# Second matmul of the expert network follows the first by three half steps instead of four and five, with its passes dealt out anew

## The chip, the cores and the metric

The kernel runs on one core of a Trainium2 chip. The core has five engines with instruction queues of their own, each worked off in order: TensorE (PE, matmuls into PSUM), ScalarE (ACT), VectorE (DVE), GpSimd (POOL) and SyncE (SP, which here issues the DMAs). Engines wait for each other by semaphores. The metric is the device time of one execution in microseconds: the median of three executions before the change is 485.01 us (484.96 to 485.11).

## The reference

Two blocks follow each other. A linear attention with a polynomial sketch gives x of 4352 tokens by 128; a mixture of four experts then works on all tokens:

```python
def phi(x):
    a = np.einsum('rd,bhsd->bhsr', S1, x)
    b = np.einsum('rd,bhsd->bhsr', S2, x)
    return np.einsum('bhsi,bhsj->bhsij', a, b).reshape(*x.shape[:-1], r * r)
q_p, k_p = (phi(q), phi(k))
kv = np.einsum('bhsf,bhsd->bhfd', k_p, v)
z = np.sum(k_p, axis=2)
attn = np.einsum('bhsf,bhfd->bhsd', q_p, kv) / (np.einsum('bhsf,bhf->bhs', q_p, z)[..., None] + 1e-06)
# (B,H,S,D) -> x: (B*S, H*D) = (4352, 128)
p = domain_probs / (domain_probs.sum(-1, keepdims=True) + 1e-09)
for e in range(4):
    h = np.maximum(x @ w1[e], 0.0)          # (4352, 1024)
    out += p[:, e:e + 1] * (h @ w2[e])      # (4352, 128)
```

B, H, S, D are 4, 4, 1088, 32, r is 8; all data are fp32.

## The kernel before

The tokens are columns. They are cut into eleven chunks (`CHUNKS`, L71): chunk 0 has 128 columns, chunk 1 has 448, chunks 2 to 7 have 512 each, then 320, 256 and 128. Each chunk passes all four experts, and of each expert the 1024 hidden rows in eight blocks of 128. Two blocks make a **step**, so an expert has four steps (`NP`) and a chunk sixteen (`NQ`); the loop at L1084 runs over all steps, numbered through: step 32 is the first of chunk 2. In a step, `f` (0 to 3) is the place in its expert and `j` (0 or 1) the block.

One step issues the first product of its own two blocks, x @ w1, in `first` (L861), and the second product, h @ w2, of an earlier step, in `second` (L945). `LA` = 2: before the change, step i carries the second product of step i - 2. Between the two blocks of `first` a callback `between` is called, so a step has a **middle** (after block 0) and an **end** (after block 1). The middle takes block 0 of step i - 2, the end block 1. If step i - 2 is its expert's last, step i is a **closing step**: the middle takes both blocks, `close` (L1077) gathers the result, and the loop goes on at once with `continue`, with nothing at its end.

Chunks 0 and 10 (`plain`) and chunk 1 (`whole`) work in fp32. In chunks 2 to 9 the fp32 products are put together from single-pass fp32r matmuls on operands that are split into parts. For the first product (any block): L911 (wa, xa) and L912 (wb, xb) into a PSUM bank, then ACT scales the bank in place (L913), and a block later `third` (L926) adds L931 (wd, xd). Then comes the relu. For even blocks (`in_three`) it makes three parts: ha by ACT (L935), hb by DVE (L936), hc by DVE (L937, listed as `hd` in the profile). For odd blocks ACT makes one fp32 tile `hid` (L943). The second product of an even block is L994 (va, ha) and L995 (vb, hb) into a first output bank o0, and one pass (vd, hc) into a second bank o1 by L1001; that of an odd block is an fp32 matmul, issued as two instructions, into o1, by L1001 too. Passes into o1 wait in a list `o1_next` until block 1 of a step when k is 0, otherwise they are issued at once.

`gather` (L1022) closes an expert: ACT copies o0, scaled, to the tile `ev` (L1030), DVE adds o1 (L1031), POOL multiplies by the gate and adds to `total` (L1035, L1037, L1038). It is a generator that is drawn on by `next(ending)` at the end of steps that aren't closing: first it loads the gates of the next chunk (L340), and for the last expert, two draws later, `turn_back` (L1006) has DVE turn the total into the tile `ob` (L1010) and SP store it by four DMAs (L1013).

The tiles `ev` and `ob` have one buffer each. `scaled` (L702) uses the same two, under the tags "ev" and "ob", for casts by ACT (L706) that POOL reads (L710). That is how the split weights are made: `weight_parts` and `second_weight_parts` are spread by `to_part` over steps 16 to 39, after `first` and ahead of what comes at the step's end. The last two casts of this kind stand in step 36. Four steps ahead of a chunk's end `token_parts` (L753) splits the next chunk's x in the same manner.

The attention (`front`, `keys`, `queries`, `attend`) is cut into pieces, which `work()` deals out after each block of `first`, at a rate worked out from what later chunks need. They put matmuls on PE (L226, L410, L666) and products, shuffles and transposes on DVE (L425, L535, L669 to L679), and DMAs on SP (x goes out to DRAM at L643 and back into a ring at L652). All order is the order of the program: the schedule is manual, and each engine takes its instructions as they are written.

Of the kernel before, what the change touches and what calls it, by code (L numbers as in the profile page):

```python
# [8 lines left out]
F32 = mybir.dt.float32  # L9
# [4 lines left out]
ACTF = mybir.ActivationFunctionType  # L14
# [10 lines left out]
def kernel(  # L25
# [24 lines left out]
    nc = tc.nc  # L50

    P = 128
    HP = 64
    B, H, S, D = q.shape
    E, DM, F = w1.shape
# [5 lines left out]
    FB = F // P  # L61
    NQ = E * FB // 2
    QW = 512
    CW = 512
    GE = 160
    LA = 2
    SK, KS = 2, 1
# [11 lines left out]
    mpool = ctx.enter_context(tc.tile_pool(name="moe", bufs=2))  # L79
# [66 lines left out]
    def second_weight(e, b):  # L146

        at = split_at(b)
        return w2_of[e, 0 if in_three(b) else 1][:, DM * at : DM * (at + 1)]

    def in_three(b):
        return b % SK < KS

    def split_at(b):
        return (b % SK - (0 if in_three(b) else KS)) * NK + b // SK
# [540 lines left out]
    R12 = 2.0 ** -12  # L696
# [28 lines left out]
    w2_parts = {}  # L725
# [111 lines left out]
    steps = [(m, kq) for m in range(NC) for kq in range(NQ)]  # L837
    hid, acc, total = {}, {}, {}
    NP = FB // 2

    def plain(m):
        return m in (0, NC - 1)
# [102 lines left out]
    def second(i, j=None):  # L945

        m, kq = steps[i]
        n, (e, f) = CHUNKS[m], divmod(kq, NP)
        hd = hid[i] if j == 0 else hid.pop(i)
        if plain(m):  # L950
# [3 lines left out]
            for j in range(2):  # L954
                for _ in range(2):
# [4 lines left out]
                        start=(f == j == 0),  # L960
                        stop=(f == NP - 1 and j == 1),
# [16 lines left out]
        if whole(m):  # L978
            if f == 0 and j == 0:
                acc[m, e] = None, psum(ps_o, f"o{e % 2}")  # L980
            for j in range(2) if j is None else (j,):
                k = 2 * f + j
                o1 = acc[m, e][1][:, 0:n]
                nc.tensor.matmul(o1, second_weight(e, k), hd[j], start=(k == 0), stop=(k == FB - 1))  # L984
            return
        if f == 0 and j in (0, None):
            acc[m, e] = psum(ps_o, "o0"), psum(ps_o, "o1")
        o0, o1 = (o[:, 0:n] for o in acc[m, e])
        for j in range(2) if j is None else (j,):
            k = 2 * f + j  # L990
            if in_three(k):
                w = slice(DM * split_at(k), DM * (split_at(k) + 1))
                (va, vb, vd), (ha, hb, hc) = w2_parts[e], hd[j]
                nc.tensor.matmul(o0, va[:, w], ha, start=(k == 0), stop=False)  # L994
                nc.tensor.matmul(o0, vb[:, w], hb, start=False, stop=(k == FB - SK + KS - 1))  # L995
                o1_next.append((vd[:, w], hc))
            else:
                o1_next.append((second_weight(e, k), hd[j]))
            if k:
                for x, (w, h) in enumerate(o1_next):  # L1000
                    nc.tensor.matmul(o1, w, h, start=(k == 1 and x == 0), stop=(k == FB - 1 and x == len(o1_next) - 1))  # L1001
                o1_next.clear()

    o1_next = []

    def turn_back(m, src):  # L1006

# [14 lines left out]
    def gather(m, e):  # L1022

        n = CHUNKS[m]
        ev = mpool.tile([P, CW], F32, tag="ev", bufs=1, name="ev")
        o0, o1 = acc.pop((m, e))
        if o0 is None:
            nc.scalar.copy(ev[:, 0:n], o1[:, 0:n])
        else:
            nc.scalar.activation(ev[:, 0:n], o0[:, 0:n], ACTF.Copy, scale=1.0 + R12)  # L1030
            nc.vector.tensor_tensor(out=ev[:, 0:n], in0=ev[:, 0:n], in1=o1[:, 0:n], op=ALU.add)  # L1031
        g = gate.pop((m, e))[:, 0:n]
        if e == 0:
            total[m] = mpool.tile([P, CW], F32, tag="total", bufs=1, name="total")
            nc.gpsimd.tensor_tensor(out=total[m][:, 0:n], in0=ev[:, 0:n], in1=g, op=ALU.mult)  # L1035
        else:
            nc.gpsimd.tensor_tensor(out=ev[:, 0:n], in0=ev[:, 0:n], in1=g, op=ALU.mult)  # L1037
            nc.gpsimd.tensor_tensor(out=total[m][:, 0:n], in0=total[m][:, 0:n], in1=ev[:, 0:n], op=ALU.add)  # L1038
        yield
        if not plain(m + 1):  # L1040
            load_gates(m + 1, [e])
        if e == E - 1:
            yield
            yield

            for _ in range(0 if m + 2 < NC else 4):
                yield
            turn_back(m, total.pop(m)[:, 0:n])
# [28 lines left out]
    def close(i):  # L1077

        nonlocal ending
        ended = gather(steps[i][0], steps[i][1] // NP)  # L1080
        next(ended)
        ending = chain(ending, ended)

    for i in range(len(steps) + LA):  # L1084
        if i < len(steps):
# [15 lines left out]
                    credit[0] -= 1  # L1101
                    piece()

            parted = i >= LA and not plain(steps[i - LA][0]) and not plain(m)
            closing = parted and steps[i - LA][1] % NP == NP - 1

            def between(j):

                if closing:
                    second(i - LA)  # L1110
                    close(i - LA)
                else:
                    second(i - LA, j)

            first(i, work, between if parted else None)
            for parts_of in to_part.get(i, ()):
                next(parts_of, None)
            if kq == NQ - 4 and 0 < m < NC - 2:
# [13 lines left out]
        if i == LA:  # L1132

            made_hp[3] = psum(ps_h, "h")
            for c in (0, HP):
                half_columns(3, made_hp[3], c)
        if i >= LA:
            parted = i < len(steps) and parted
            mm, kk = steps[i - LA]
            if parted and closing:  # L1140
                continue
            second(i - LA, 1 if parted else None)
            if kk % NP == NP - 1 and not plain(mm):
                close(i - LA)
            else:
                next(ending, None)

# [1 line left out]
_INS = ["q", "k", "v", "S1", "S2", "moe_domain_probs", "moe_w1", "moe_w2"]  # L1149
# [26 lines left out]
```

## Time and profile before

| what | value |
|---|---|
| median of three executions | 485.01 us |
| profiled execution | 485.2 us |
| its span, first to last instruction | 483.4 us |
| PE busy | 471.4 us (98%) |
| ACT busy | 331.2 us (69%) |
| DVE busy | 327.2 us (68%) |
| POOL busy | 141.9 us (29%) |
| granted TensorE clock | 1.00 |

In a timeline a row has start and duration in us, engine, line, operation, output and inputs, the shape, and in square brackets the idle time before it and what ended it. A matmul's duration overlaps the next one's start, so distances between starts tell what PE takes. A row of the waits says who waited for whom, then the sum in us, how often, and the longest. In the rows by stretch, busy time and number of instructions of PE, weight loads, DVE, ACT and POOL are followed by the granted clock, the mean busy share of the DMA engines, and GB/s. Chunk 2 begins at 81.0 us, chunk 3 at 138.5, chunk 4 at 193.7, chunk 5 at 247.8, chunk 6 at 301.6, chunk 7 at 353.8, chunk 8 (320 columns) at 404.6 and chunk 9 (256) at 437.2, by their first L911.

### The profile page before, as it was taken

To read this page: it belongs to the slowest core of one execution; us is meant where nothing else is said; L and a number is where in the kernel's file an instruction comes from. 1 tells how busy PE (TensorE), PEld (TensorE's weight loads), DVE (VectorE), ACT (ScalarE), POOL (GpSimd) and SP (SyncE) were. 2 spreads that over 40 slices of the span, in tenths; PEclk is the share of its full clock that TensorE was granted. 3 is DMA by queue.
4 is the path that set the end of the run, shared out by engine and by line. 5 is a ranking of instruction groups with operands and counts; after the bars stand their busy time and mean duration, and the time that the engine had idled before them with its cause. 6 is when DMAs were issued, how large, how long until landed. Compare 5 with 4: busy or idle time off the path is not lost.

```text
span 483.4 us, 8071 instructions
## 1 busy us (share of the span) xinstructions
PE 471.4 (98%) x2845; PEld 330.8 (68%) x2845; DVE 327.2 (68%) x615; ACT 331.2 (69%) x696; POOL 141.9 (29%) x149
## 2 busy tenths in 40 slices
PE   8999999989999999999999999999999999999997
PEld 5965555656666676666666676667666666888987
DVE  6833250696877769687887669597877686765652
ACT  4366676876857777676857777676877686888841
POOL 5134478432222124211322124212331032232120
PEclk9999999999999999999999999999999999999999
DMA  7827204411101212411103210013102100120710
GB/s 225 273 69 159 66 22 87 97 42 23 44 23 49 45 44 65 118 24 41 41 23 65 45 33 24 22 17 45 38 24 58 29 14 15 34 57 22 244 34 18
DMA packets 45472, 29.19 MB, mean 60 GB/s; under 512 B 26264, under 2 KB 40952, under 8 KB 45432
## 3 DMA queue, kind: packets, MB, share of 16 engines
q1 hardware_dynamic: 45416, 28.68, 23.6%
q8 instruction: 22, 0.36, 0.3%
q14 instruction: 18, 0.15, 0.1%
q10 hardware_dynamic: 16, 0.00, 0.0%
HBM read 24.42 MB, written 4.24 MB: 59 GB/s over the span
## 4 chain that ended last, share of the span: by engine, by line
PE 66%; DVE 6%; ACT 5%; issue 2%; ACTq 0%; DVEq 0%
PE o L1001 23%; PE h L931 10%; PE h L912 8%; PE h L911 8%; PE o L994 5%; PE o L995 5%; ACT h L913 3%; PE n L226 2%; PE h L226 2%; PE o L226 1%; DVE qp L535 1%; DVE hd L937 1%; DVE kp L425 1%; PE f L666 1%; DVE hb L936 1%
## 5 line engine op out<-in xcount | busy, mean ns | idle before, releaser
L913 ACT ACTIVATE h<-h 128x512 f32<-128x512 f32 (+2 forms) x256 | 138.0, 539 | 100.6 <-PE h L912 91.6
L936 DVE SCALAR_TENSOR_TENSOR hb<-h,ha 128x512 fp32r<-128x512 f32 (+2 forms) x128 | 80.8, 631 | 92.3 <-ACT ha L935 91.8
L911 PE MATMUL h<-xa,wa 128*128 128x512 f32 (+2 forms) x256 | 140.5, 549 | 0.0
L1001 PE MATMUL o<-hid,w_sb 128*128 128x512 f32 (+2 forms) x256 | 119.2, 547 | 0.0
L937 DVE SCALAR_TENSOR_TENSOR hd<-ha,hb 128x512 fp32r<-128x512 f32 (+2 forms) x128 | 98.8, 772 | 8.4
L931 PE MATMUL h<-xd,wd 128*128 128x512 f32 (+2 forms) x256 | 98.3, 384 | 3.2 <-ACT h L913 1.5
L912 PE MATMUL h<-xb,wb 128*128 128x512 f32 (+2 forms) x256 | 94.2, 368 | 0.0
L1037 POOL TENSOR_TENSOR ev<-ev,gate 128x512 f32<-128x512 f32 (+3 forms) x27 | 31.3, 1159 | 153.8 <-DVE ev L1031 153.1
L943 ACT ACTIVATE hid<-h 128x512 f32<-128x512 f32 (+2 forms) x128 | 70.2, 548 | 0.2 <-PE h L931 0.2
L935 ACT ACTIVATE ha<-h 128x512 fp32r<-128x512 f32 (+2 forms) x128 | 69.9, 546 | 0.0
L911 PEld LDWEIGHTS h<-xa,wa 128*128 128x128 f32 x256 | 48.2, 188 | 30.1 <-issue 18.6
L912 PEld LDWEIGHTS h<-xb,wb 128*128 128x128 f32 x256 | 48.3, 189 | 29.3 <-issue 23.6
L931 PEld LDWEIGHTS h<-xd,wd 128*128 128x128 f32 x256 | 48.0, 188 | 23.7 <-ACT h L913 16.0
L1001 PEld LDWEIGHTS o<-hid,w_sb 128*128 128x128 f32 x256 | 45.9, 188 | 8.1
L1001 PE MATMUL o<-hd,vd 128*128 128x512 f32 (+2 forms) x128 | 48.3, 378 | 2.7 <-DVE ev L1031 2.7
L994 PE MATMUL o<-ha,vab 128*128 128x512 f32 (+2 forms) x128 | 50.6, 395 | 0.0
L995 PE MATMUL o<-hb,vab 128*128 128x512 f32 (+2 forms) x128 | 47.4, 370 | 0.0
L1038 POOL TENSOR_TENSOR total<-total,ev 128x512 f32<-128x512 f32 (+3 forms) x27 | 35.4, 1313 | 2.1
L535 DVE TENSOR_TENSOR qp<-qa,qb 64x512 f32<-64x512 f32 (+5 forms) x44 | 33.1, 753 | 1.0
L1035 POOL TENSOR_TENSOR total<-ev,gate 128x512 f32<-128x512 f32 (+3 forms) x9 | 10.5, 1163 | 70.3 <-issue 34.0
L1001 PEld LDWEIGHTS o<-hd,vd 128*128 128x128 f32 x128 | 24.0, 187 | 9.3 <-DVE ev L1031 4.5
L984 PE MATMUL o<-hid,w_sb 128*128 128x448 f32 x64 | 28.9, 544 | 0.0
(150 smaller groups left out, 545.4 us busy)
## 6 DMA issues: line engine op xcount, KB each, us to landing
gate<-gates SPq DMA_DIRECT2D x16, 256.0 KB
kn<-in_k_dram SPq DMA_DIRECT2D x4, 544.0 KB
vn<-in_v_dram SPq DMA_DIRECT2D x16, 128.0 KB
w_sb<-in_moe_w_dram SPq DMA_DIRECT2D x4, 512.0 KB
w_sb<-in_moe_w_dram SPq DMA_DIRECT2D x8, 256.0 KB
w_last<-in_moe_w_dram SPq DMA_DIRECT2D x4, 512.0 KB
gate<-gates SPq DMA_DIRECT2D x8, 224.0 KB
qn<-in_q_dram SPq DMA_DIRECT2D x2, 544.0 KB
```

The source lines that it names most:

```text
L535: nc.vector.tensor_tensor(out=qp[p][64 * x : 64 * x + 64, 0:n], in0=qa[64 * p : 64 * p + 64, 0:n], in1=qb[64 * p : 64 * p + 64, 0:n], op=A ...
L911: nc.tensor.matmul(g, wa[:, e, w], xa, start=True, stop=False)
L912: nc.tensor.matmul(g, wb[:, e, w], xb, start=False, stop=True)
L913: nc.scalar.activation(g, g, ACTF.Copy, scale=1.0 + R12)
L931: nc.tensor.matmul(g, w, x, start=False, stop=True, skip_group_check=True)
L935: nc.scalar.activation(ha, g, ACTF.Relu, scale=NEAR)
L936: nc.vector.scalar_tensor_tensor(out=hb, in0=g, scalar=0.0, in1=high, op0=ALU.max, op1=ALU.subtract)
L937: nc.vector.scalar_tensor_tensor(out=hc, in0=high, scalar=R12, in1=hb.bitcast(F32), op0=ALU.mult, op1=ALU.subtract)
L943: nc.scalar.activation(hid[i][j], g, ACTF.Relu)
L994: nc.tensor.matmul(o0, va[:, w], ha, start=(k == 0), stop=False)
L995: nc.tensor.matmul(o0, vb[:, w], hb, start=False, stop=(k == FB - SK + KS - 1))
L1001: nc.tensor.matmul(o1, w, h, start=(k == 1 and x == 0), stop=(k == FB - 1 and x == len(o1_next) - 1))
```

## The change

Half steps are now counted: the middle of step i is 2i, its end 2i + 1. After each `first`, its second products go into a list `due`: block 0 of a split or whole step at 2i + 3, block 1 at 2i + 4, both blocks of a plain step at 2i + 5. `behind(at)` issues all that is due. So block 0 of step i is issued at the end of step i + 1 (before: the middle of step i + 2), block 1 in the middle of step i + 2 (before: its end, or the middle if the step was closing).

In the split chunks the passes are dealt out anew. Block 0 first issues what waits in `o1_next`, then (va, ha) and, if f isn't 0, (vb, hb) into o0; its (vd, hc) always goes to `o1_next`. With f = 0, (vb, hb) waits in a new list `o0_next` until block 1, and the fp32 pass of block 1 goes to `o1_next` too, so that the expert's first writes to o1 come with block 0 of f = 1. With f = 3, block 1 issues the waiting (vd, hc) and then its fp32 pass.

The copy of o0 to `ev` by ACT is issued right after the last pass into o0, with block 0 of f = 3 (the end of the step ahead of the closing step), and no more in `gather`. `close` still comes in the middle of the closing step. The `continue` is gone: the end of a closing step issues what is due and draws on `ending`, so what `gather` does after its first `yield` comes one step earlier.

```diff
--- before.py
+++ after.py
@@ -983,25 +983,48 @@
                 o1 = acc[m, e][1][:, 0:n]
                 nc.tensor.matmul(o1, second_weight(e, k), hd[j], start=(k == 0), stop=(k == FB - 1))
             return
-        if f == 0 and j in (0, None):
+        if f == 0 and j == 0:
             acc[m, e] = psum(ps_o, "o0"), psum(ps_o, "o1")
-        o0, o1 = (o[:, 0:n] for o in acc[m, e])
-        for j in range(2) if j is None else (j,):
-            k = 2 * f + j
-            if in_three(k):
-                w = slice(DM * split_at(k), DM * (split_at(k) + 1))
-                (va, vb, vd), (ha, hb, hc) = w2_parts[e], hd[j]
-                nc.tensor.matmul(o0, va[:, w], ha, start=(k == 0), stop=False)
-                nc.tensor.matmul(o0, vb[:, w], hb, start=False, stop=(k == FB - SK + KS - 1))
-                o1_next.append((vd[:, w], hc))
+            begun_o[:] = [False, False]
+        k = 2 * f + j
+
+        def into(o, w, h, last=False):
+            nc.tensor.matmul(acc[m, e][o][:, 0:n], w, h, start=not begun_o[o], stop=last)
+            begun_o[o] = True
+
+
+
+
+        if j == 0:
+            for args in o1_next:
+                into(1, *args)
+            o1_next.clear()
+            w = slice(DM * split_at(k), DM * (split_at(k) + 1))
+            (va, vb, vd), (ha, hb, hc) = w2_parts[e], hd[j]
+            into(0, va[:, w], ha)
+            if f == 0:
+                o0_next.append((vb[:, w], hb))
             else:
-                o1_next.append((second_weight(e, k), hd[j]))
-            if k:
-                for x, (w, h) in enumerate(o1_next):
-                    nc.tensor.matmul(o1, w, h, start=(k == 1 and x == 0), stop=(k == FB - 1 and x == len(o1_next) - 1))
+                into(0, vb[:, w], hb, f == NP - 1)
+            o1_next.append((vd[:, w], hc))
+            if f == NP - 1:
+                evs[m, e] = mpool.tile([P, CW], F32, tag="ev", bufs=1, name="ev")
+                nc.scalar.activation(evs[m, e][:, 0:n], acc[m, e][0][:, 0:n], ACTF.Copy, scale=1.0 + R12)
+            return
+        for args in o0_next:
+            into(0, *args)
+        o0_next.clear()
+        x = second_weight(e, k), hd[j]
+        if f == 0:
+            o1_next.append(x)
+        else:
+            if f == NP - 1:
+                for args in o1_next:
+                    into(1, *args)
                 o1_next.clear()
-
-    o1_next = []
+            into(1, *x, f == NP - 1)
+
+    o0_next, o1_next, begun_o, evs = [], [], [False, False], {}
 
     def turn_back(m, src):
 
@@ -1022,12 +1045,12 @@
     def gather(m, e):
 
         n = CHUNKS[m]
-        ev = mpool.tile([P, CW], F32, tag="ev", bufs=1, name="ev")
         o0, o1 = acc.pop((m, e))
         if o0 is None:
+            ev = mpool.tile([P, CW], F32, tag="ev", bufs=1, name="ev")
             nc.scalar.copy(ev[:, 0:n], o1[:, 0:n])
         else:
-            nc.scalar.activation(ev[:, 0:n], o0[:, 0:n], ACTF.Copy, scale=1.0 + R12)
+            ev = evs.pop((m, e))
             nc.vector.tensor_tensor(out=ev[:, 0:n], in0=ev[:, 0:n], in1=o1[:, 0:n], op=ALU.add)
         g = gate.pop((m, e))[:, 0:n]
         if e == 0:
@@ -1080,6 +1103,21 @@
         ended = gather(steps[i][0], steps[i][1] // NP)
         next(ended)
         ending = chain(ending, ended)
+        closed[0] = i
+
+
+    due, closed = [], [None]
+
+    def behind(at):
+
+        was = closed[0]
+        while due and due[0][0] <= at:
+            _, i, j = due.pop(0)
+            second(i, j)
+            m, kq = steps[i]
+            if kq % NP == NP - 1 and j == 1:
+                close(i)
+        return closed[0] != was
 
     for i in range(len(steps) + LA):
         if i < len(steps):
@@ -1101,18 +1139,8 @@
                     credit[0] -= 1
                     piece()
 
-            parted = i >= LA and not plain(steps[i - LA][0]) and not plain(m)
-            closing = parted and steps[i - LA][1] % NP == NP - 1
-
-            def between(j):
-
-                if closing:
-                    second(i - LA)
-                    close(i - LA)
-                else:
-                    second(i - LA, j)
-
-            first(i, work, between if parted else None)
+            first(i, work, lambda j: behind(2 * i))
+            due.extend([(2 * i + 5, i, None)] if plain(m) else [(2 * i + 3, i, 0), (2 * i + 4, i, 1)])
             for parts_of in to_part.get(i, ()):
                 next(parts_of, None)
             if kq == NQ - 4 and 0 < m < NC - 2:
@@ -1134,16 +1162,8 @@
             made_hp[3] = psum(ps_h, "h")
             for c in (0, HP):
                 half_columns(3, made_hp[3], c)
-        if i >= LA:
-            parted = i < len(steps) and parted
-            mm, kk = steps[i - LA]
-            if parted and closing:
-                continue
-            second(i - LA, 1 if parted else None)
-            if kk % NP == NP - 1 and not plain(mm):
-                close(i - LA)
-            else:
-                next(ending, None)
+        if not behind(2 * i + 1):
+            next(ending, None)
 
 # ---- launch: one core; inputs and outputs as the reference has them ----
 _INS = ["q", "k", "v", "S1", "S2", "moe_domain_probs", "moe_w1", "moe_w2"]
```

## The prediction

> **What bounds the kernel now.** I read the page first: busy shares, then the chain that ended last.
>
> ```profile
> PE 471.4 (98%) x2845; PEld 330.8 (68%) x2845; DVE 327.2 (68%) x615; ACT 331.2 (69%) x696; POOL 141.9 (29%) x149
> ...
> PE 66%; DVE 6%; ACT 5%; issue 2%; ACTq 0%; DVEq 0%
> ```
>
> TensorE (PE) is the bound, and a third of the chain leaves it, so there are stalls to win. In the timeline of PE I then took the distance between starts. A 512-column single-pass matmul (L911, L912, L931, L994, L995, L1001 on `hd`) starts 0.23 us after the one before; an fp32 pair (L1001 on `hid`) takes 0.86 us. An undisturbed step is 9 x 0.23 + 0.86 = 2.93 us; L994 at 354.85 and 357.80 are 2.95 us apart. So between closings there is nothing to win by reordering, only something to lose. The stalls sit at the closings, where an expert's last step ends. PE at one of them:
>
> ```profile
> 117.00 0.39 PE L912 MATMUL h<-xb,wb 128*128 128x512 f32 x1
> 117.23 0.39 PE L931 MATMUL h<-xd,wd 128*128 128x512 f32 x1
> 117.46 0.39 PE L911 MATMUL h<-xa,wa 128*128 128x512 f32 x1
> 117.69 0.39 PE L912 MATMUL h<-xb,wb 128*128 128x512 f32 x1
> 118.12 0.50 PE L931 MATMUL h<-xd,wd 128*128 128x512 f32 x1
> 118.46 0.70 PE L666 MATMUL f<-qT,sq 128*128 128x320 f32 x2
> ```
>
> The second product is all done in the middle of that step, so only three matmuls lie between L912 at 117.00 and its own L931, which needs ACT's L913 in between. It starts 0.43 after 117.69 instead of 0.23, and the next start is 0.34 later instead of 0.23: 0.20 + 0.11 = 0.31 us lost. L912 to its L931 takes at least 118.12 - 117.00 = 1.12 us; four matmuls between would fill 5 x 0.23 = 1.15.
>
> The other place is chunk 2's start, where ACT and POOL still make weight parts. ACT, POOL, DVE and SP there, each from its own timeline:
>
> ```profile
> 98.22 0.59 ACT L935 ACTIVATE ha<-h 128x512 fp32r<-128x512 f32 x1
> 98.70 1.16 ACT L706 ACTIVATE tw<-w_sb 128x512 f32<-128x512 f32 x2
> 99.74 0.60 ACT L913 ACTIVATE h<-h 128x512 f32<-128x512 f32 x1
> ...
> 101.61 0.60 ACT L1030 ACTIVATE ev<-o 128x512 f32<-128x512 f32 x1 [0.76 <-POOL vab L710]
> ...
> 99.93 1.65 POOL L710 TENSOR_TENSOR vab<-tw 128x512 fp32r<-128x512 f32 x1 [7.14 <-ACT tw L706]
> ...
> 102.16 0.65 DVE L1010 STREAM_TRANSPOSE ob<-total 128x448 f32<-128x448 f32 x1
> ...
> 102.83 1.95 SPq L1013 DMA_DIRECT2D out_dram<-ob  x4
> ```
>
> L706 at 98.70 (step 36) casts into the single buffers "ob" and "ev". L1030 uses "ev" next and waits for POOL to have read it; L1010 uses "ob" next, one step's end later. DMA around L1013's stores:
>
> ```profile
> 102.80:103.50 0.70, 0.70 (x3) 0.62 (x4) 0.67 (x2) 0.70 (x2) 0.00 (x0) 1.00 0.00 0
> 103.50:105.85 2.35, 1.98 (x8) 0.93 (x7) 2.28 (x4) 2.23 (x5) 0.81 (x1) 1.00 0.62 98
> 105.85:107.00 1.15, 1.15 (x5) 0.51 (x3) 1.14 (x2) 0.00 (x0) 1.15 (x2) 1.00 0.05 14
> ```
>
> The last columns (DMA share, GB/s) show the four stores moving data until 105.85, 3.0 us after L1010 ended at 102.81.
>
> **The change, part by part.** The sum is made against the profiled execution: 485.2 us (span 483.4), 0.2 above the median of 485.0.
>
> *Steady steps: 0.* Same matmuls, same number of changes between pair and single passes. The pair moves to the middle of a step, the three singles to its end; six singles or more still lie between L912 and its L931 (1.61 us against 1.12).
>
> *Closings of 512 columns: -4.0.* In the new order the closing step ends with one L994 of the next expert (va alone, vb is held back), so four matmuls lie between, and the stall goes. A half step later only vb's pass stands in the middle (two passes before), so again four; there ACT must also fit L935, its starts are 0.49 apart, and L931 comes 0.05 late by my count, with or without the 0.11 restart. So each closing gains 0.31 less 0 to 0.16; I take 0.25, as some have attention matmuls in that spot. Between 117 and 386 us I count fifteen such closings outside the third expert: 15 x 0.25 = 3.75. The closing of chunk 1 (L931 at 89.21 waits for ACT) gains one filler, 0.25.
>
> *Third expert's closings: +0.3.* There `token_parts` puts two casts (0.52 each) on ACT, and the copy of the first bank, now half a step earlier, comes behind them and ahead of L913: counted from the second L912 of the step before, L913's result comes after 3.65 us, PE would be there after 3.39. Four of the six then wait for DVE's add L1031 anyway, so there it costs 0; two lose 0.15.
>
> *Chunks of 320 and 256 columns: +0.4.* A filler is worth 0.145 or 0.117 there, less than the stalls of 0.30 and 0.33; two smaller stalls with a restart each replace one.
>
> *The wait for the second bank: 0.* `PE o L1001 <- DVE ev L1031` costs 2.7 us in 5 places. Though first writes wait a step, they stand at the same spot: eleven singles after the closing pair in both orders. Nothing gained.
>
> *The operands' cover: +0.45.* L995 needs DVE's hb. Until now the earliest waiter was the L911 that takes over the buffer; the new L995 stands 0.40 us before it and needs 0.24 for its weight load, so a step stalls if hb ends less than 0.64 before L911. Outside closing steps, where vb's place is later, I find one (hb ends 353.45, L911 starts 353.75): 0.34 + 0.11. hc gets 0.9 us more cover; `hid` loses 0.7 of at least 1.28 us between the end of L943 and the L911 that reuses its bank, at 512 columns.
>
> *`next(ending)` no longer skips the closing step: gate loads and the output's turn come one step earlier.* On SP, gate loads wait for POOL's L1037 (they do now, 161.2 us in sum) and now stand ahead of some xd stores and ring loads; these are read 10 us later or more (ring load 172.06, L758 181.93), so 0, or up to 3 us if that cover were gone. POOL has ended by the turn (413.30 against about 415 in the 320-column chunk): 0.
>
> *The same, in chunk 2: +3.0.* Chunk 1's turn now lands at the end of step 35, before step 36's casts, instead of behind them. Then L1010 runs at about 98.33 to 98.98 (after the shuffle at 97.59), its stores hold "ob" until 98.98 + 3.03 = 102.0, and ACT, in order, stands at L706 from 98.7 until 102.1. Queued behind: both casts (to 103.2), POOL's L710 (1.65, to 104.95), and, new, the copy of the first bank at the end of step 36, which needs "ev" (105.0 to 105.6); behind it L913 (to 106.1), for which PE's L931 waits: 106.2 instead of 101.28, 4.9 late. The next two L931 meet an ACT with five activations queued 0.5 apart, 0.6 more, and three restarts 0.3: 5.8. What PE loses there now falls away, because DVE and ACT catch up meanwhile: 0.79 (L931 at 102.75), 0.26 (104.27), 0.55 (L1001 at 105.05, waiting for L1031), 1.11 (L226 at 108.60, waiting for L535) and 0.1 of restarts, 2.8. Net 3.0. Bounds: 0 if the stores were done before ACT arrives, 5.8 if nothing falls away. I take 3.0 because DVE's own rows (L535 took 1.68 beside POOL, 0.68 without) end by 111, before PE comes back to L226 at 111.7.
>
> The Trainium skill, "DMA: Bandwidth & Descriptors", section "Anatomy of one DMA", says a transfer has a fixed cost of about 2 us, mostly the receipt of its last write, before its semaphore moves: a rule against reusing a buffer soon after a store. By it, the last of four issues (104.3) would free "ob" at about 106.4, 0.6 later than the row, and my sum would be 485.8. The page describes another issuing path; the row decides.
>
> Sum: -4.0 + 0.3 + 0.4 + 0.45 + 3.0 = +0.15: 485.35 for a profiled execution, 485.2 for the median.
>
> **The rivals.**
> - *Slower: the stall of step 36 is not paid back.* It decides if DVE is held by it too: L1031, hb and L535 then slip with ACT, and PE finds L226 late again. For: DVE's add needs the copy at 105.6. Against: 0.9 us of margin by my count. 485.2 + 2.8 = 488.0.
> - *Faster: the collision is cheap*, since stores release "ob" early or the turn comes in time. Against: the 3.0 us of the stores are in the rows. 485.2 - 3.0 = 482.2.
> - *Slower by cover: hb.* DVE is full beside the attention pieces; if, with PE no longer stalled at closings, six steps rather than one meet a late hb, 5 x 0.45 = 2.3: 487.5.
> - *Closings gain only 0.1 each:* 485.2 + 15 x 0.15 = 487.4; I put it with the rival above.
>
> **How the numbers follow.** This kernel tells 0.2%, 1.0 us, from no change. Forecast 0.47 (own range 484.1 to 486.4): of it 0.05 faster, 0.37 same, 0.05 slower. Stall not paid back 0.15, slower. Collision cheap 0.20, 0.19 of it faster. Late hb or small gains 0.18: 0.05 same, 0.13 slower. Together 0.24 faster, 0.43 same, 0.33 slower. The range 483.0 to 488.0 leaves out half of the cheap case and half of the unpaid one.
>
> **What would show it.** Right: L1010 first at about 98.3, ACT idle before L706 for 3 us or more, released by the stores, PE idle about 5 us near 101 to 106; L931 no longer waiting 0.2 at closings; L1001 still waiting for L1031 about 3 us; L995 hardly waiting. Wrong: no gap in ACT at 98.7 (then 3 us faster), or PE waiting for hb in many steps.

## Result and profile after

The changed kernel takes 490.67 us (median of four executions, 490.18 to 491.57), the old one 485.0: a ratio of 1.0119, 95% interval 1.0101 to 1.0136. The profiled execution took 491.09 us, its span is 489.3 us. The forecast was 485.2 with a range up to 488.0. From the page: busy shares, the granted clock over forty slices, the chain that ended last.

```profile
PE 472.6 (97%) x2845; PEld 332.1 (68%) x2845; DVE 322.8 (66%) x615; ACT 327.4 (67%) x696; POOL 142.6 (29%) x149
...
PEclk9999999988999999999999999999999999999999
...
PE 81%; ACT 5%; issue 5%; DVE 5%; POOL 3%; DMA 0%; ACTq 0%; POOLq 0%; DVEq 0%
```

TensorE's share of the chain rose from 66% to 81% and yet the kernel is slower: fewer small stalls, and a few large ones. They are in the waits (who waited for whom, us in sum, how often, the longest), before:

```profile
PE o L1001 <- DVE ev L1031: 2.7, 5, 1.0
...
PE h L931 <- ACT h L913: 1.5, 6, 0.6
```

and after:

```profile
PE h L931 <- ACT h L913: 6.0, 3, 4.9
...
PE o L992 <- DVE ev L1054: 4.1, 5, 1.2
```

(L992 is now every pass of the second product, L1012 the copy of the first bank, L1054 DVE's add, L1033 and L1036 the turn and its stores; before they were L994, L995 and L1001, and L1030, L1031, L1010, L1013.)

To see where the time came from, I compared the two traces at points of equal work: the fp32 pair that ends each expert's second product. How much later the new kernel reaches each of them, counted from the one before, gives this account (below, such a difference is called an equal-work step):

| place | forecast, us | measured, us |
|---|---|---|
| end of chunk 1, start of chunk 2 | -0.25 | +1.33 |
| turn of chunk 1's output against the casts of step 36 | +3.0 | +5.0 |
| closings of 512 columns outside the third expert | -3.75 | -3.1 |
| third expert's closings | +0.3 | +2.0 |
| chunks of 320 and 256 columns | +0.4 | +0.5 |
| hb's cover | +0.45 | 0 |
| sum | +0.15 | +5.7 |

**A closing of chunk 2.** PE's timeline, after:

```profile
123.46 0.39 PE L912 MATMUL h<-xb,wb 128*128 128x512 f32 x1
123.69 0.40 PE L931 MATMUL h<-xd,wd 128*128 128x512 f32 x1
123.93 0.40 PE L992 MATMUL o<-ha,vab 128*128 128x512 f32 x1
124.16 0.39 PE L911 MATMUL h<-xa,wa 128*128 128x512 f32 x1
124.39 0.40 PE L912 MATMUL h<-xb,wb 128*128 128x512 f32 x1
124.63 0.45 PE L931 MATMUL h<-xd,wd 128*128 128x512 f32 x1
124.92 0.70 PE L666 MATMUL f<-qT,sq 128*128 128x320 f32 x2
```

L912 at 123.46 to its own L931 at 124.63 are now five starts, and the stall of 0.2 before L931 is gone. That part came as told.

**The collision in chunk 2.** ACT, DVE, SP and POOL, each from its own timeline, after:

```profile
104.14 1.15 ACT L706 ACTIVATE tw<-w_sb 128x512 f32<-128x512 f32 x2 [3.24 <-DVE qa L679]
106.66 0.60 ACT L1012 ACTIVATE ev<-o 128x512 f32<-128x512 f32 x1 [1.37 <-POOL vab L710]
107.16 0.59 ACT L913 ACTIVATE h<-h 128x512 f32<-128x512 f32 x1
...
100.02 0.63 DVE L1033 STREAM_TRANSPOSE ob<-total 128x448 f32<-128x448 f32 x1
...
100.67 1.94 SPq L1036 DMA_DIRECT2D out_dram<-ob  x4
...
105.37 1.26 POOL L710 TENSOR_TENSOR vab<-tw 128x512 fp32r<-128x512 f32 x1 [10.90 <-ACT tw L706]
```

This is the chain that the prediction told: turn, stores, ACT standing at L706 (3.24 us; the releaser named, L679, had long ended, so it was the stores), POOL's L710, the copy, L913. What PE made of it:

```profile
102.51 0.40 PE L912 MATMUL h<-xb,wb 128*128 128x512 f32 x1
107.80 0.80 PE L931 MATMUL h<-xd,wd 128*128 128x512 f32 x1 [4.90 <-ACT h L913]
108.39 0.63 PE L992 MATMUL o<-ha,vab 128*128 128x512 f32 x1
108.82 0.63 PE L911 MATMUL h<-xa,wa 128*128 128x512 f32 x1
109.25 0.63 PE L912 MATMUL h<-xb,wb 128*128 128x512 f32 x1
```

4.90 us idle, as forecast. But then single passes start 0.43 us apart instead of 0.23. The rows by stretch (granted clock third from the end) say why:

```profile
104.00:106.00 2.00, 0.00 (x0) 0.00 (x0) 0.79 (x2) 1.15 (x2) 0.63 (x1) 1.00 0.01 4
106.00:108.00 2.00, 0.20 (x1) 0.20 (x2) 0.69 (x1) 1.34 (x3) 0.63 (x1) 0.70 0.00 0
108.00:110.00 2.00, 2.00 (x5) 1.61 (x6) 0.69 (x1) 1.86 (x5) 1.38 (x2) 0.50 0.00 0
...
112.00:114.00 2.00, 2.00 (x5) 1.00 (x4) 1.60 (x3) 0.77 (x2) 0.00 (x0) 0.59 0.04 11
```

In the idle stretch the TensorE clock fell to half (in finer rows at 106.8, 3.9 us after L912 ended), and it stayed there until 113.6, 5.8 us after PE worked again. From 108.39 to 113.16 PE did nine singles and a pair, 2.5 us of work at full clock (9 x 0.23, and 0.46 from the pair's start to the next), in 4.8 us. The Trainium skill, "TensorE: Matmul & The Clock Gate", section "What's actually happening", states both halves of this: after an idle window of about 3.4 us the array falls to half clock, and it needs about as long of sustained work to get out. Here the fall fits, 3.9 us after L912 ended at 102.91, and the return took longer than the page's figure, 5.8 us. It is a rule that spoke against this change, and the prediction did not weigh it.

**The end of chunk 1.** PE, after:

```profile
81.93 1.02 PE L984 MATMUL o<-hid,w_sb 128*128 128x448 f32 x2 [0.84 <-ACT hid L900]
...
90.91 0.50 PE L931 MATMUL h<-xd,wd 128*128 128x512 f32 x1 [0.93 <-ACT h L913]
```

ACT waits 3.42 us for POOL at a weight cast shortly before (3.41 in the old kernel), and makes `hid` (L900) behind it. In the old kernel `hid` was used a half step later, and no L984 near it waited. The second wait, 0.93, was 0.23 in the old kernel: its L913 stands behind the copy of chunk 1's result, which waits for POOL in both (0.59 and 0.57 us).

**A third expert's closing.** ACT, DVE and PE in the old kernel, at the end of chunk 2:

```profile
127.82 0.63 ACT L706 ACTIVATE tw<-ring 128x512 fp32r<-128x512 f32 x1
...
131.96 0.69 DVE L1031 TENSOR_TENSOR ev<-ev,o 128x512 f32<-128x512 f32 x1
...
128.56 1.02 PE L1001 MATMUL o<-hid,w_sb 128*128 128x512 f32 x2
...
132.70 0.51 PE L1001 MATMUL o<-hd,vd 128*128 128x512 f32 x1 [0.28 <-DVE ev L1031]
```

ACT, DVE, POOL and PE there, after:

```profile
134.66 0.63 ACT L706 ACTIVATE tw<-ring 128x512 fp32r<-128x512 f32 x1
...
135.79 1.48 DVE L535 TENSOR_TENSOR qp<-qa,qb 64x320 f32<-64x320 f32 x1
...
137.90 0.88 DVE L535 TENSOR_TENSOR qp<-qa,qb 64x320 f32<-64x320 f32 x1
138.81 0.69 DVE L1054 TENSOR_TENSOR ev<-ev,o 128x512 f32<-128x512 f32 x1
...
135.37 1.55 POOL L710 TENSOR_TENSOR xb<-ring,tw 128x512 fp32r<-128x512 f32 x1 [7.31 <-ACT tw L706]
137.00 1.43 POOL L710 TENSOR_TENSOR xd<-xa,xb 128x512 fp32r<-128x512 f32 x1
...
134.78 1.02 PE L992 MATMUL o<-hid,w_sb 128*128 128x512 f32 x2
...
139.55 0.51 PE L992 MATMUL o<-hd,vd 128*128 128x512 f32 x1 [0.73 <-DVE ev L1054]
```

DVE's add comes 4.15 us after the second cast of `token_parts` (L706) in the new kernel and 4.14 in the old one. The closing pair comes 4.03 us before the add (134.78); in the old kernel it came 3.40 before (128.56 to 131.96). Block 0's passes now stand a half step ahead of the pair, and so the pair starts 0.12 us after that cast instead of 0.74, while the casts and what they do to DVE stayed at their step. So PE arrives at the second bank earlier and waits longer.

### The profile page after: what moved, and what is told of

Same layout as the page of the kernel before. It is cut to its first block, busy times and chain, and to the rows that moved or that the text cites. A ratio compares the mean times of both kernels' runs of the same rounds, so it can differ in the third digit from the quotient of the medians.

```text
span 489.3 us, 8084 instructions
## 1 busy us (share of the span) xinstructions
PE 472.6 (97%) x2845; PEld 332.1 (68%) x2845; DVE 322.8 (66%) x615; ACT 327.4 (67%) x696; POOL 142.6 (29%) x149
## 4 chain that ended last, share of the span: by engine, by line
PE 81%; ACT 5%; issue 5%; DVE 5%; POOL 3%; DMA 0%; ACTq 0%; POOLq 0%; DVEq 0%
PE o L992 33%; PE h L931 10%; PE h L912 9%; PE h L911 9%; PE h L898 4%; PE h L226 4%; PE o L984 3%; PE o L226 3%; PE n L226 3%; ACT h L913 1%; DVE kp L425 1%; PE f L666 1%; ACT ha L935 1%; DVE qp L535 1%; POOL vab L710 1%
## 5 line engine op out<-in xcount | busy, mean ns | idle before, releaser
L913 ACT ACTIVATE h<-h 128x512 f32<-128x512 f32 (+2 forms) x256 | 139.6, 545 | 105.5 <-PE h L912 105.1
L936 DVE SCALAR_TENSOR_TENSOR hb<-h,ha 128x512 fp32r<-128x512 f32 (+2 forms) x128 | 80.8, 631 | 102.2 <-ACT ha L935 101.2
L911 PE MATMUL h<-xa,wa 128*128 128x512 f32 (+2 forms) x256 | 129.9, 508 | 0.0
L992 PE MATMUL o<-hid,w_sb 128*128 128x512 f32 (+2 forms) x256 | 120.1, 551 | 0.0
L931 PE MATMUL h<-xd,wd 128*128 128x512 f32 (+2 forms) x256 | 101.1, 395 | 6.5 <-ACT h L913 6.0
L937 DVE SCALAR_TENSOR_TENSOR hd<-ha,hb 128x512 fp32r<-128x512 f32 (+2 forms) x128 | 95.9, 749 | 9.1 <-DVE hb L936 0.5
L912 PE MATMUL h<-xb,wb 128*128 128x512 f32 (+2 forms) x256 | 94.9, 371 | 0.0
L931 PEld LDWEIGHTS h<-xd,wd 128*128 128x128 f32 x256 | 48.4, 189 | 28.2 <-ACT h L913 21.0
L912 PEld LDWEIGHTS h<-xb,wb 128*128 128x128 f32 x256 | 48.5, 190 | 24.7 <-issue 18.0
L992 PE MATMUL o<-ha,vab 128*128 128x512 f32 (+2 forms) x128 | 59.4, 464 | 0.0
L992 PE MATMUL o<-hd,vd 128*128 128x512 f32 (+2 forms) x128 | 49.6, 387 | 4.1 <-DVE ev L1054 4.1
L992 PEld LDWEIGHTS o<-hid,w_sb 128*128 128x128 f32 x256 | 46.0, 189 | 8.1 <-issue 0.2
L992 PE MATMUL o<-hb,vab 128*128 128x512 f32 (+2 forms) x128 | 49.7, 389 | 0.0
L1061 POOL TENSOR_TENSOR total<-total,ev 128x512 f32<-128x512 f32 (+3 forms) x27 | 37.5, 1388 | 2.1
L535 DVE TENSOR_TENSOR qp<-qa,qb 64x512 f32<-64x512 f32 (+5 forms) x44 | 32.6, 740 | 0.9
L992 PEld LDWEIGHTS o<-hd,vd 128*128 128x128 f32 x128 | 24.2, 189 | 10.0 <-DVE ev L1054 6.1
L992 PEld LDWEIGHTS o<-hb,vab 128*128 128x128 f32 x128 | 24.3, 190 | 9.7 <-issue 5.5
L992 PEld LDWEIGHTS o<-ha,vab 128*128 128x128 f32 x128 | 24.4, 191 | 9.0 <-issue 6.0
```

Of the source, the lines that this page charges most:

```text
L535: nc.vector.tensor_tensor(out=qp[p][64 * x : 64 * x + 64, 0:n], in0=qa[64 * p : 64 * p + 64, 0:n], in1=qb[64 * p : 64 * p + 64, 0:n], op=A ...
L911: nc.tensor.matmul(g, wa[:, e, w], xa, start=True, stop=False)
L912: nc.tensor.matmul(g, wb[:, e, w], xb, start=False, stop=True)
L913: nc.scalar.activation(g, g, ACTF.Copy, scale=1.0 + R12)
L931: nc.tensor.matmul(g, w, x, start=False, stop=True, skip_group_check=True)
L936: nc.vector.scalar_tensor_tensor(out=hb, in0=g, scalar=0.0, in1=high, op0=ALU.max, op1=ALU.subtract)
```

## Experiments

Theory A: the turn's collision, with the clock it costs, makes most of the slowdown, the rest is lost cover at the end of chunk 1 and at the third expert's closings. Theory B (the rival): the new dealing of the passes itself costs, at every closing, and the collision is a small part. Medians of the old kernel beside these runs were 485.2 to 485.4 us.

**Clock alone.** The changed kernel with matmuls whose result nobody uses in the place where PE idles:

```
             nc.scalar.activation(g, g, ACTF.Copy, scale=1.0 + R12)
+            if i == 2 * NQ + 5 and j == 1:
+                wp = psum(ps_h, "h")
+                for _ in range(20):
+                    nc.tensor.matmul(wp[:, :], warm[:, 0:P], warm[:, :], start=True, stop=True)
             third()
```

> The changed kernel, with twenty extra bf16 matmuls of 512 columns (results unused) put on TensorE ahead of the L931 that waits 4.9 us in step 37, so that TensorE is not idle there. Nothing else changes: ACT and DVE are late as before. Theory A (the stall at chunk 2's start, and behind it the granted clock that fell to 0.50 for some 6 us, cost 5.0 us together, of which the clock about 3): the granted clock stays at 1.00, the wait stays, the time falls by 2.5 to 3.5 us to about 487.5. Rival B (the clock in the profile is only a record, and the time goes to late operands all over): no change, 490 to 491.

Measured 489.22 us (489.16 to 490.08), ratio to the old kernel 1.0077 (1.006 to 1.0094). The granted clock in the same stretch:

```profile
104.00:106.00 2.00, 1.94 (x10) 0.91 (x10) 1.76 (x4) 0.83 (x2) 0.00 (x0) 1.00 0.23 36
...
108.00:110.00 2.00, 1.50 (x7) 0.84 (x6) 0.69 (x1) 2.00 (x5) 0.91 (x1) 1.00 0.04 8
```

With the clock held at 1.00 the collision costs 2.95 us by the equal-work points instead of 5.00. The 2.05 us between them are the clock (2.04 by the two ratios to the old kernel, 1.45 by the medians; this profiled execution was 1 us late from its start, ahead of the edit). More work made the kernel faster, though less than expected; and 2.95 is the forecast's 3.0, which had counted idle time but no clock.

**The turn alone, undone.** The changed kernel with chunk 1's turn one draw later:

```
-            for _ in range(0 if m + 2 < NC else 4):
+            for _ in range((m == 1) if m + 2 < NC else 4):
                 yield
```

> The changed kernel, with the turn of chunk 1's output one step later (the end of step 36, where it was before the change). Theory A: ACT no longer waits for the stores; what is left is the wait of the copy of the first bank for POOL's L710, about 2 us of PE stall of which most is paid back, and the clock stays at 1.00: 485.5 to 486.5. Rival B (late operands everywhere, the stall is paid back in any case): over 489.

Measured 486.39 us (485.61 to 489.75), ratio 1.0022 (1.0006 to 1.0039): 4.3 us of the 5.7 are gone by the medians, 4.9 by the equal-work points. The equal-work step of that expert is +0.09 instead of +5.00, all others are as before. What is left there, in ACT's timeline:

```profile
100.80 1.15 ACT L706 ACTIVATE tw<-w_sb 128x512 f32<-128x512 f32 x2
103.60 0.60 ACT L1012 ACTIVATE ev<-o 128x512 f32<-128x512 f32 x1 [1.65 <-POOL vab L710]
```

L706 no longer waits, but the early copy still stands behind POOL.

**The turn alone, in the old kernel.** Only that draw moved one step earlier:

```
         if e == E - 1:
             yield
-            yield
+            if m != 1:
+                yield
```

> The kernel before the change, with one thing changed: chunk 1's output is turned one step earlier, ahead of the casts of step 36. Theory A: ACT idles some 3 us ahead of L706 here too; L913 of step 37 comes about 2.5 us late, the second one about 3.5; 1.9 us is paid back: 486.0 to 487.5, or 489 if the clock falls as well. Rival C (the stores do not hold ACT by themselves, the new place of the second product does): 485.0, unchanged.

Measured 488.62 us (487.55 to 488.86), ratio 1.006 (1.0044 to 1.0077). One yield makes the old kernel 3.2 us slower, with nothing else changed. ACT stands 3.56 us at L706, PE 2.62 at L931, and the clock falls here too:

```profile
104.00:107.00 3.00, 2.15 (x5) 1.24 (x6) 0.85 (x2) 2.61 (x6) 1.57 (x2) 0.59 0.00 0
```

**Chunk 1 followed as before.** The turn late, and chunk 1's second product four and five half steps behind, both blocks of a closing in one place, as in the old kernel:

```
+            late = whole(m)
+            last = late and kq % NP == NP - 1
             due.extend(
-                [(2 * i + 5, i, None)] if plain(m) else [(2 * i + 3, i, 0), (2 * i + 4, i, 1)]
+                [(2 * i + 5, i, None)] if plain(m) else [(2 * i + 3 + late, i, 0), (2 * i + 4 + late - last, i, 1)]
             )
```

> As e2_turn_late, and the second product of chunk 1 follows its first by four and five half steps again, with both blocks in the middle of a closing step. Theory A: 1.3 us were lost between the last closing of chunk 1 and the first of chunk 2, because L984 met a hid that ACT had not made; this goes: 1.0 to 1.5 us faster than e2_turn_late. Rival D (those 1.3 us come from the casts alone): equal to e2_turn_late within 0.3.

Measured 485.14 us (484.5 to 486.04), ratio 0.9991 (0.998 to 1.0001). The steps at chunk 1's end went from +0.47 and +0.86 to -0.01 and -0.23, and neither the wait of L984 for `hid` nor the 0.93 at L931 is left. So the distance at which chunk 1's second product follows, with the place of its closing's blocks, was the cause of both. That the wait for `hid` brings on the second one is not shown: the run undoes both together. With turn and chunk 1 undone, what remains of the change is as fast as the old kernel: theory B, that the new dealing itself costs at every closing, falls with this run.

**The copy at chunk 2's start.** In addition, the first expert of chunk 2 copies its bank in `gather`, as before:

```
-            if f == NP - 1:
+            if f == NP - 1 and (m, e) != (2, 0):
                 evs[m, e] = mpool.tile(...)
```

> The turn late and chunk 1 followed as before, as in the run of both (485.1), and in addition the copy of the first bank of chunk 2's first expert issued in the middle of the closing step, where the old kernel had it, instead of at the end of step 36. Theory: what is left at chunk 2's start is the copy standing behind POOL's last weight part (1.6 to 2 us of ACT, 1.8 of PE at one L931, with a dip of the granted clock after it). Then the equal-work point of that expert goes from +1.0 (profiled) back to about 0 or below, and the time to 484.0 to 484.5. Rival: the later copy makes DVE's add, and by it the first write to the second bank, late by as much, and the time stays at 485.1.

Measured 484.47 us (484.12 to 485.97), ratio 0.9983 (0.9974 to 0.9991). The 0.99 us that the profile of the run before had lost there is gone (step +0.09). All further versions of the new order but the next start from this one.

**All copies in the closing step.** From the run that is as fast as the old kernel, the early copy is taken back everywhere:

```
-            if f == NP - 1:
+            if f > NP:
                 evs[m, e] = mpool.tile(...)
```

> The kernel with the late turn and chunk 1 followed as before (485.1), with the copies of the first bank of all experts in the middle of the closing step, where the old kernel had them, half a step later than the change puts them; the rest of the change stays. Theory: the early copy stands ahead of L913 behind the two casts of token_parts, and makes that L931 0.15 to 0.23 late; with the copy in the closing step these stalls (five at 512 columns, the ones at 320 and 256) go, as does the stall at chunk 2's start: 1 to 2.5 us faster, 482.6 to 484.1. Rival: the copy then stands ahead of the L913 of the closing step's second block, whose L931 comes four matmuls later, and each closing loses 0.2 to 0.3 again (27 of them, up to 6 us, 487 to 490); or the add waits for the copy and the second bank's first write is later by up to 0.5 at each closing.

Measured 485.24 us (485.02 to 486.84), ratio 1.0 (0.999 to 1.0009): neither the gain nor the loss that was expected. The stalls of L931 behind the casts did go at 512 columns, and a new one came that neither theory had named. The next expert's first pass overwrites the bank that the copy (L1056 here) reads:

```profile
130.48 0.50 PE L992 MATMUL o<-ha,vab 128*128 128x512 f32 x1 [0.34 <-ACT ev L1056]
```

Such waits sum to 3.1 us in 7 places, five of them 0.34 to 0.35 us at third experts' closings, where the next chunk's two casts stand ahead of the copy. There the early copy belongs to the early first pass.

**The held pass.** vb's pass of an expert's first block at once, the rest as in the run of 484.47:

```
-            if f == 0:
-                o0_next.append((vb[:, w], hb))
-            else:
-                into(0, vb[:, w], hb, f == NP - 1)
+            into(0, vb[:, w], hb, f == NP - 1)
```

> The kernel with turn, chunk 1 and chunk 2's first copy as in the old one (484.5), with one part of the new dealing undone: vb's pass of an expert's first block is issued at once, right behind va's, instead of a half step later. Theory of the closings: held back, it is the fourth matmul between L912 and L931 a half step after the closing; without it three matmuls lie there and the stall of 0.31 us returns at each closing of 512 columns: 15 x 0.25 to 0.31, 3.8 to 4.7 us slower, 488 to 489. Rival: the closings gain comes from the earlier pair and the copy, not from this pass, and the time stays at 484.5; or the earlier L992 waits for DVE's hb in addition (then `PE o L992 <- DVE hb L936` shows it).

Measured 484.9 us (484.59 to 486.37), ratio 0.9997 (0.9988 to 1.0006). Only 0.4 us were lost, not four. Where no attention matmul stands near, three matmuls do leave a stall, as here in chunk 7:

```profile
385.96 0.40 PE L912 MATMUL h<-xb,wb 128*128 128x512 f32 x1
386.33 0.50 PE L931 MATMUL h<-xd,wd 128*128 128x512 f32 x1
386.67 0.39 PE L992 MATMUL o<-hd,vd 128*128 128x512 f32 x1
```

(0.37 after L912 instead of 0.23.) It comes back at eight of the sixteen closings of 512 columns outside the third expert. At the other eight a matmul of the attention (L666 or L410) lies between L912 and its L931, as an L666 in chunk 2. By equal-work steps against the old kernel, the first eight gain 0.12 us in sum here and 0.95 with the pass held; the other eight gain 2.56 here, 0.32 each, and 2.14 with it held. So the mechanism holds, but the held pass is little of the gain: most of it is that the stall's place moved to half steps in which other work fills it. Holding the pass or not moves the time by 0.4 us in all.

**Where the casts of the next chunk stand.** `token_parts` one step later, behind the third expert's closing, in the new order and, as a control, in the old kernel:

```
-            if kq == NQ - 4 and 0 < m < NC - 2:
+            if kq == NQ - 3 and 0 < m < NC - 2:
```

> The kernel of the run before this in the list, with token_parts one step later (after the third expert's closing instead of ahead of it). Theory: the wait of the second bank's first write for DVE's add at the third expert's closings (4.1 us in 5 places with the change) comes from the casts and POOL's L710 beside DVE, whose L535 took 1.48 us there against 0.48 alone; moved behind the closing, those waits and the 0.2 at each of these L931 go, and the time falls by 2.5 to 4 us, to 480.5 to 482. Rival 1: DVE is late there from its own attention work, and the time stays (484 to 484.5). Rival 2: xb and xd then come too late for the next chunk's first step, and the wait only moves to L912 and L931 there (485 or more).

> The kernel before the change with token_parts one step later and nothing else. The old kernel has 2.7 us of waits for DVE's add in 5 places. If POOL's and ACT's work for token_parts is their cause in both kernels: 2 to 2.8 us faster, 482.2 to 483. If the wait belongs to the new order of passes: no change, 485.

Measured in the new order 483.14 us (482.97 to 484.61), ratio 0.9957 (0.9944 to 0.9971); in the old one 486.15 us (485.7 to 486.8), ratio 1.0013 (1.0005 to 1.0022). The waits of the second bank for the add went in both but for 0.4 and 0.2 us. But the two casts now stand ahead of another L913, for whose result L931 waits 5.3 us in 8 places in the new order, 5.4 in 13 in the old one. By equal-work points that is a gain in chunks 1 to 5, where the attention loads DVE, and a loss after them. For the control the expectation was plainly wrong: the old kernel had less to win at these closings, and pays as much.

**The later place in chunks 1 to 5 only**, again in both kernels:

```
-            if kq == NQ - 4 and 0 < m < NC - 2:
+            if kq == NQ - (3 if m < 6 else 4) and 0 < m < NC - 2:
```

> The new order with chunk 1's turn late, chunk 1 followed as before, chunk 2's first copy in the closing step, and token_parts one step later in chunks 1 to 5 only (in all chunks it gave 483.1). By the equal-work points of that run, the later place gained 0.1, 0.9, 0.5, 0.7 and 0.7 us in chunks 1 to 5 and lost 0.7, 0.5 and 0.3 in chunks 6 to 8, where the attention no longer loads DVE and only ACT's two casts stand ahead of L913. If the two add up independently: 484.5 - 2.9 = 481.6. Rival: the loss of the later chunks belongs to the earlier lead, and they lose it in any case: 483.

> The kernel before the change with token_parts one step later in chunks 1 to 5 only. With the later place in all chunks it was 0.7 us slower than without; its equal-work points gave -0.1, -0.7, +0.1, -0.4 and -0.1 in chunks 1 to 5. If these add up: 484.2. It tells how much of the gain of the kernel above belongs to the place of token_parts alone and how much to the new order of passes.

Measured in the new order 482.17 us (481.61 to 482.81), ratio 0.9937 (0.9924 to 0.9949); in the old one 484.41 us (483.74 to 485.39), ratio 0.998 (0.9971 to 0.9989). The same move is worth 2.3 us in the new order (against 484.47) and about 0.9 in the old: the 1.4 us between them belong to the new order's earlier pair, near the 1.7 by which the forecast of these closings was off. The equal-work steps of the third experts' closings in chunks 2 to 5 say the same: with the casts later they are -0.70, +0.13, -0.36 and -0.07 in the new order and -0.73, +0.13, -0.36 and -0.07 in the old one. So with the casts behind the closing the two orders no longer differ there. DVE at the closing of chunk 2's third expert in the new order (L1057 is the add):

```profile
130.20 0.49 DVE L535 TENSOR_TENSOR qp<-qa,qb 64x320 f32<-64x320 f32 x1
...
131.31 0.48 DVE L535 TENSOR_TENSOR qp<-qa,qb 64x320 f32<-64x320 f32 x1
131.83 0.69 DVE L1057 TENSOR_TENSOR ev<-ev,o 128x512 f32<-128x512 f32 x1
```

The same two L535 that took 1.48 and 0.88 beside POOL take 0.49 and 0.48, 1.39 less; the add comes 2.64 us after its pair (129.19) instead of 4.03, 1.39 less. So it was POOL's L710 beside DVE that made the add late.

The Trainium skill, "SBUF — State Buffer", section "SBUF: two separate sides", has it that a DVE instruction with two SBUF inputs and a GpSimd instruction that reads SBUF lock one pair of ports for their whole length, so that one blocks the other. The trace agrees: the L535 that began at 135.79, 0.42 us into an L710 of 1.55 us, took 1.00 us longer than alone, about the rest of that L710 (1.13).

**The two casts apart.** What the later place still cost was L931 waiting for L913 behind two casts. In chunks 1 to 5 they are put on two successive steps, `tw` first (behind chunk 5 only the order of the two changes):

```
     def token_parts(m):
...
-        nc.scalar.activation(xa[:, 0:n], x, ACTF.Copy, scale=R12 * NEAR)
         minus(xb[:, 0:n], x, scaled("ew", x, NEAR, F32R))
+        if m < 7:
+            yield
+        nc.scalar.activation(xa[:, 0:n], x, ACTF.Copy, scale=R12 * NEAR)
         minus(xd_[:, 0:n], xa[:, 0:n].bitcast(F32), xb[:, 0:n].bitcast(F32))
         xparts[m] = xa, xb, xd_
+        yield
...
-                token_parts(m + 1)
+                to_part.setdefault(i + 1, []).append(token_parts(m + 1))
+                next(to_part[i + 1][-1])
```

> The kernel with token_parts one step later in chunks 1 to 5 (482.2), with the two casts of token_parts (ACT L706 and L758, 0.52 us each) on two successive steps' ends instead of one behind the other, in those chunks. There, L931 now waits 3.8 us in 6 places for L913 behind the two casts. If that wait is the two casts in ACT's line, one cast alone leaves 0.52 less at each of five places, and the second place costs at most 0.2: 1 to 2.5 us faster, 479.7 to 481.2. Rival: ACT is full enough that the second cast costs as much at its own place, and the time stays at 482.2; or xd comes too late for the next chunk's first L931, slower by up to 1 us a chunk.

Measured 480.04 us (479.88 to 480.39), ratio 0.9892 (0.9876 to 0.9909), about 5.2 us faster than the old kernel. ACT in chunk 2:

```profile
131.15 0.63 ACT L706 ACTIVATE tw<-ring 128x512 fp32r<-128x512 f32 x1
131.67 0.60 ACT L916 ACTIVATE h<-h 128x512 f32<-128x512 f32 x1
...
133.66 0.65 ACT L761 ACTIVATE xa<-ring 128x512 fp32r<-128x512 f32 x1
```

(L916 is L913 there, L761 the cast L758, L934 is L931.) The wait of L931 for L913 is down from 3.8 us in 6 places to

```profile
PE h L934 <- ACT h L916: 1.7, 6, 0.3
```

and that for the add is 0.4 us in 2 places, as before this edit. The old kernel was not run with its casts apart, so how much of these last 2.1 us (482.17 to 480.04) needs the new order stays open.

## Why the prediction was wrong

- **"The same, in chunk 2: +3.0" failed in its size.** Every instruction of its chain came in the order told, with the idle time of 4.90 us it gave for L931. The term "0.6 more, and three restarts 0.3" that followed that idle time is what was mis-sized: it priced PE's restart at full clock and had no term for the clock, which had fallen to 0.50. Clock held, the step is +2.95; as it was, +5.0. Of the terms before it, the 3.03 us for which the stores hold "ob" were 3.49 (100.65 to 104.14). The turn's part is shown from both sides, 4.3 us undone in the new kernel and 3.2 us done alone in the old one.
- **The closing of chunk 1, "gains one filler, 0.25", was wrong in sign.** It became 1.33 us with the start of chunk 2. The sum costed the shorter follow distance only at 512 columns; for chunk 1 it has no row of when `hid` is ready, though ACT's 3.41 us wait for POOL stood in the profile. Restoring the distance gave 1.25 us back.
- **"The wait for the second bank: 0" and "Third expert's closings: +0.3" failed together:** +2.0. "Eleven singles after the closing pair in both orders" is right, and not the point: the waiting is for an add whose time is fixed by the step of `token_parts`, and the pair moved earlier against it. Four of the six, in chunks 2 to 5, make 1.8 of it, and the wait for the add stands at each of these. The copy behind the casts (0.26 forecast per closing, some 0.2 measured at L931) is hidden by that wait there, as forecast: at 139.55 PE starts right behind the add (138.81 + 0.69), whatever it lost before. The run with all copies in the closing step took these stalls away, had 0.34 at the copy instead, and left the equal-work steps of the third experts' closings at 2.1 us in sum.
- **Closings, -3.75 forecast, -3.1 measured:** right in kind and near in size. The reason given, a fourth matmul between L912 and L931, was tested by taking the held pass away. It is worth 0.8 us at the eight closings where no attention matmul fills the place, and costs 0.4 at the other eight, which gain their 0.31 without it.
- **Steady steps 0, narrow chunks +0.4, and gate loads 0** held (measured 0, +0.5, nothing seen). **hb, +0.45,** did not come: the waits hold only 0.4 us of a weight load of L992 for L936, and no late matmul.
- The rival "the stall of step 36 is not paid back" gave 488.0 by DVE's lateness; it fell short, and by another cause. What was at fault was to cost a stall of 5 us by its length alone.

## What to carry to other kernels

A gap of several us on TensorE costs more than its length: price the half-clock stretch behind it as a term of its own, and prefer a late store or turn to one that holds a shared buffer ahead of an in-order engine. When a change pulls one stream of work forward, list what stays anchored to the old step (casts, copies, adds) and recount each wait between the two, for every kind of chunk, even where the count of instructions between is the same. Small waits of this kind are worth chasing by moving the anchored work too: here the change lost 5.7 us as it stood and won 5.2 with five further edits, of which the move of the casts alone won 0.9 in the old kernel too.

## What the runs showed of the hardware

- The clock fell behind shorter idle stretches than the 4.9 us here. With an idle of 2.6 us at L931 in the old kernel with the early turn it read 0.59 in the next 3 us. In the run of 485.14 a wait of 1.8 us at the same L931 was followed by 0.55, while the run of 486.39, with a wait of 1.8 us too, kept 1.00. The program alone does not decide it: of the ten executions of the kernel of 485.14, three have a mean clock of 0.996, which is what 3.4 us at half clock make of it, and seven have 1.00. What does decide stays open.
- The clock was at half for 6.8 us in the changed kernel (106.8 to 113.6), and for 3.4 us in the old one with the early turn (104.6 to 108.0) and in the run of 485.14 (104.3 to 107.7). In that last one it fell 1.45 us after PE had started again.
- Four stores from SP (0.23 MB) released their buffer 3.5 us after the transpose that filled it (100.65 to 104.14), against 3.0 read from the DMA rows of the old kernel.
- Twenty more matmuls on TensorE, in the place of an idle stretch, made the whole program faster, by 1.45 us by the medians and 2.05 by the equal-work points.
